# Per-unit leads and delays, feature matrices on VectorE, and an early weight load in an FNet and squared-ReLU kernel

## The chip, the core and the metric

The kernel runs on one core of a Trainium2 chip. A core has TensorE (PE in the profile; PEld is its weight load), VectorE (DVE), ScalarE (ACT), GpSimd (POOL) and SyncE (SP), which run their own instruction streams and meet by semaphores, and 16 DMA engines. DMAs are issued on the queues of SP, ACT and POOL. The metric is the time of one execution on the device in microseconds; of several runs, the median.

## What is computed

```python
def _attn_ref(x):                      # x: 8 x 3008 x 256, float32
    X = np.fft.fft(x, axis=1)
    X = np.fft.fft(X, axis=2)
    return X.real.astype(np.float32)

def _moe_ref(x, w_in, w_out):          # x: 24064 x 256, w_in: 256 x 2048, w_out: 2048 x 256
    h = np.maximum(x @ w_in, 0.0)
    return (h * h @ w_out).astype(np.float32)
```

The second function takes the first one's result, its eight batches of 3008 rows laid end to end. The output is 24064 x 256 in float32.

## The kernel before

**The transform.** The rows of a batch are folded by symmetry (`fold_ops`): sums `u` and `v` and features `w`, all on VectorE, from an `x4` tile that holds one batch and its reversed rows. The reversed rows come by indirect DMAs of POOL (`gather`, line 101), the others by direct ones (SP for batch 0, POOL for the rest). A DFT over the folded rows (`stage1_ops`, matmuls into `pf`) with cosine and sine tables `cosT`, `sinT` gives for each batch the two 128-row arrays `pt` and `qt`, of 1505 columns each. The tables have two blocks of columns, block 0 for even frequencies and block 1 for odd ones, and are computed by the kernel: range reduction on VectorE (`red`), sines on ScalarE (`trig`), and mirrored halves (`mir`, on ScalarE for block 0, on VectorE for block 1), which are scaled by per-partition vectors `alt`, `nalt`, `alt1`, `nalt1`.

**The weights.** The transform along the 256 features is not applied to the data. It is multiplied into `w_in` (`gmat`): four quarters of 512 columns are loaded (`load_w_in`, on the queue of ScalarE), cast (`gcast`) and multiplied with the feature matrices `csD`, which `dmats` makes. The results are `G1`, `G2` and `G3`, the last being `G2` with signs (`gneg`). `w_out` is loaded by POOL as float16 (`load_w_out`).

**The main loop.** The 8 x 1505 columns are cut into 25 chunks: two of 256, 22 of 512, one of 264. A chunk is passed in units: one unit is 128 of the 2048 hidden rows (256 in the two small chunks), so a full chunk has 16 units. All units in order are the steps of the loop. A unit needs the product for the columns and for their mirror images. The letter in `KINDS` says how it is made:

- `r`: `x_front` streams `G1` and `G2` into a PSUM tile `xb`, ScalarE writes the relu of it (line 607); two steps later `x_back` adds the `G3` product and ScalarE writes the mirror's relu (line 675). Three sets of matmuls.
- `v`: the same, with the mirror's relu on VectorE (line 672).
- `d`: `x_take` streams `G1` alone; VectorE forms T = X - 2 xb (line 653), where the edge product X is made by `edge` (line 634, VectorE) out of one broadcast row. Two steps later `x_back` adds the `G2` product, ScalarE writes the relu (line 663), and a mirror add on VectorE (line 664) writes the mirror's relu from xb and T. Two sets of matmuls.
- `q`: like `d`, but ScalarE copies -2 xb (line 650) and POOL adds X (line 651).
- `p`: like `d`, but POOL makes the edge product. No unit of the kernel before has it.

When the two units of a pair are there, their `h` tile is squared, on VectorE (line 687) or, for the pairs in `SQA`, on ScalarE in two halves (lines 684 and 685). Then come the 128-row matmuls with `wout16` into `po` (`mm2_ops`), which are spread over the steps of the next chunk, the copy to `os` (line 558) and the store on SP's queue.

**What sets the order.** The schedule is by hand: each engine's instructions run in the order in which the Python code issues them. Each step issues the front of its unit, half of its share of `po` matmuls, the back of the unit of two steps ago, the other half, the mirror adds that are due (`DLAG`: one step after their back), the edge product of the next step's unit, the squares that are due (three steps behind the back, one in the small chunks), and then what `side` has for this step: gmat, table operations, folds, DFT matmuls, each placed by a fraction of its batch's steps (`FOLD`, `ST1`).

**The start.** Lines 689 to 733 are the ramp, before the loop. `dmats` runs first and puts four operations and the eight of `alt_vecs` on POOL; the table operations of block 0 follow on VectorE and ScalarE in two halves, then `dmats_fin`, `sgn_vecs` on POOL, a memset of `ez`, two operations of block 1's tables, the mirrors of block 0 with the four weight loads after the second of them, the folds of batch 0 with `load_w_out` and then the load of batch 1 among them. Ten matmuls named `warm` on the zeroed `ez`, whose result nobody reads, run ahead of the first real ones, and one more behind `gmat(0)`.

Of the kernel before, what the change touches and what calls it, by code (L numbers as in the profile page):

```python
# [14 lines left out]
ALU = mybir.AluOpType  # L15
# [4 lines left out]
R23 = float(2.0 ** 23)  # L20
# [4 lines left out]
def kernel(  # L25
# [7 lines left out]
    nc = tc.nc  # L33
    B, S, D = x.shape
    _, F = moe_w_in.shape
    P = 128
# [129 lines left out]
    nalt1 = vec("nalt1")  # L166

    def alt_vecs():
        nc.gpsimd.tensor_scalar(out=alt, in0=pidx, scalar1=0.5, scalar2=-0.25, op0=ALU.mult, op1=ALU.add)
        nc.gpsimd.tensor_scalar(out=alt2, in0=alt, scalar1=R23, scalar2=None, op0=ALU.add)  # L170
        nc.gpsimd.tensor_scalar(out=alt2, in0=alt2, scalar1=R23, scalar2=None, op0=ALU.subtract)
        nc.gpsimd.tensor_tensor(alt, alt, alt2, op=ALU.subtract)
        nc.gpsimd.tensor_scalar(out=alt, in0=alt, scalar1=4.0, scalar2=None, op0=ALU.mult)
        nc.gpsimd.tensor_scalar(out=nalt, in0=alt, scalar1=-1.0, scalar2=None, op0=ALU.mult)
        nc.gpsimd.tensor_scalar(out=alt1, in0=top, scalar1=2.0, scalar2=alt[:, 0:1], op0=ALU.mult, op1=ALU.add)
        nc.gpsimd.tensor_scalar(out=nalt1, in0=alt1, scalar1=-1.0, scalar2=None, op0=ALU.mult)

    def sgn_vecs():
        nc.gpsimd.tensor_scalar(out=sgn, in0=pidx, scalar1=P - 1.5, scalar2=None, op0=ALU.is_lt)
        nc.gpsimd.tensor_scalar(out=s3, in0=sgn, scalar1=-2.0, scalar2=None, op0=ALU.mult)  # L180
        nc.gpsimd.tensor_scalar(out=sgn, in0=sgn, scalar1=2.0, scalar2=-1.0, op0=ALU.mult, op1=ALU.add)
        nc.gpsimd.tensor_scalar(out=nsgn, in0=sgn, scalar1=-1.0, scalar2=None, op0=ALU.mult)

    def absval(o, i):
        ts(out=o.bitcast(I32), in0=i.bitcast(I32), scalar1=0x7FFFFFFF, scalar2=None,
# [4 lines left out]
    sinD = csD[:, :, 1, :]  # L190

    def dmats():
        pv = nc.gpsimd
        t, m = jm[:, 1], jm[:, 2]
        pv.tensor_scalar(out=m, in0=jrow, scalar1=pidx[:, 0:1], scalar2=None, op0=ALU.mult)
        pv.tensor_scalar(out=t, in0=m, scalar1=1.0 / D, scalar2=R23, op0=ALU.mult, op1=ALU.add)
        pv.tensor_scalar(out=t, in0=t, scalar1=R23, scalar2=-float(D),
                         op0=ALU.subtract, op1=ALU.mult)
        pv.tensor_tensor(m, m, t, op=ALU.add)
        pv.memset(csD[:, 0, 0, P - 1 : P], 1.0)  # L200
        alt_vecs()

        def fin():
            absval(t, m)
            nc.vector.tensor_copy(csD[:, 0, 1, P - 1 : P], alt)
            act(csD[:, 0, 1, 0 : P - 1], m[:, 0 : P - 1], AF.Sin, bias=0.0, scale=wD)
            act(csD[:, 0, 0, 0 : P - 1], t[:, 0 : P - 1], AF.Sin, bias=hpi[:, 0:1], scale=-wD)

        def hi():
            act(csD[:, 1, :, 0:P:2], csD[:, 0, :, 0:P:2], AF.Copy, bias=0.0, scale=-1.0)  # L210
            nc.scalar.copy(csD[:, 1, :, 1:P:2], csD[:, 0, :, 1:P:2])
        return fin, hi
# [85 lines left out]
    def gcast(c, cp):  # L298
        cp(win16(c), wst[c])
# [188 lines left out]
        g += n  # L488


    KINDS = ["vrvrrrrrrrrrrrrr"] + ["rrrrvrrvrrrrrrrr"] + ["rvrrvvrrrvrrrrrr"] + ["rrrrrrrqdrrdrrrr"] + ["rdqqrrqrqrrrdrrq"] + ["rrrrddrrqrqrdqqq"] + ["rrrrrrqqqddrrdqd"] + ["rrdrqqdrrdrrqrqr"] + ["rqdddrqrrdrdrrdr"] + ["qddrqrdrrrdqddrr"] + ["drddqrdrrrddqrdr"] + ["qrrdrdddrrdrqrqr"] + ["drrdrqdrrddrdrqr"] + ["rrqdrdqrqqrrrddr"] + ["rrddqdqqrrqqdqqq"] + ["rrrrrrqqqddqrqrd"] + ["qdrdddrdqdrqdqrr"] + ["drdqqqrdqrqdrqqr"] + ["qdqqdqrqqrqdrqrq"] + ["dddrdqrdrqqdrqdq"] + ["dddrdqdrqrqdrddr"] + ["qdqqdqrdqrqdrqqr"] + ["qrqddqrqqrqdrqdr"] + ["qdqqdqvqqrqdqrdr"] + ["rddrdddddrdrdrdd"]
    SQA = [()] + [(3,)] + [(2, 6)] + [(0, 4, 5)] + [(0, 2, 5, 6)] + [(0, 4, 6)] + [(2, 3, 7)] + [(4, 6)] + [(5, 7)] + [(2, 5, 6)] + [(3, 7)] + [(0, 2, 6)] + [(0, 2, 5, 6)] + [(2, 4, 6)] + [(3,)] + [(1, 4, 6, 7)] + [(1, 2, 6)] + [(1, 4, 6)] * 2 + [(1, 4, 5, 6, 7)] + [(1, 4, 6)] * 3 + [(1, 4, 6, 7)] + [(0, 1, 6)]

    gE = const.tile([P, NFC], F16, name="gE")
    gE2 = const.tile([P, NFC], F32, name="gE2")
# [120 lines left out]
            nc.sync.dma_start(out=ebc[c][:, o : o + l],  # L616
                              in_=PQ[b][1][P - 1 : P, i : i + l].unsqueeze(1).to_broadcast([1, P, l]))

    DLAG = {'q': 1, 'd': 1, 'p': 1}
    mirrors = []  # L620
    taken = [0]
    tbuf = []
# [33 lines left out]
    def x_back(cur):  # L656
        c, u, xb, T = cur
        g0, n, nf, segs = chunks[c]
        if T is not None:
            fs = slice(u * P, (u + 1) * P)  # L660
            for (b, i, o, l) in segs:
                mm(xb[:, 0, o : o + l], G2[:, fs], PQ[b][1][:, i : i + l], False, True)
            act(r_s(c, u), xb, AF.Relu, scale=-1.0)  # L663
            mirrors.append((DLAG[KINDS[c][u]], lambda: relu_d(c, u, lambda o, i: nc.vector._custom_dve(  # L664
                TENSOR_ADD_SAT, out=o[:, 0, :], in0=xb[:, 0, i], in1=T[:, i], s0=BIG, s1=0.0))))
            return
        for j in range(nf):
            fs = slice((u * nf + j) * P, (u * nf + j + 1) * P)
            for (b, i, o, l) in segs:
                mm(xb[:, j, o : o + l], G3[:, fs], PQ[b][1][:, i : i + l], False, True)  # L670
        if KINDS[c][u] == "v":
            relu_d(c, u, lambda o, i: ts(out=o, in0=xb[:, :, i], scalar1=-1.0, scalar2=0.0,
                                         op0=ALU.mult, op1=ALU.max))
            return
        relu_d(c, u, lambda o, i: act(o, xb[:, :, i], AF.Relu, scale=-1.0))  # L675
# [14 lines left out]
    fe, fo = fold_ops(0)  # L690
    rd0, tr0, mi0 = table_ops(0)
    rd1, tr1, mi1 = table_ops(1)
    dmats_fin, dmats_hi = dmats()

    def load_w_in():
        for c in range(4):
            cs = slice(c * F // 4, (c + 1) * F // 4)
            nc.scalar.dma_start(out=wst[c],
                                in_=moe_w_in[:, cs].rearrange("(c p) f -> p c f", p=P))
# [6 lines left out]
                in_=moe_w_out[c * F // 4 : (c + 1) * F // 4, :].rearrange("(c p) o -> p c o", p=P))  # L706

    for h in range(2):
        for f in rd0[5 * h : 5 * h + 5] + (tr0[5:] if h else tr0[:5]):
            f()  # L710
    dmats_fin()
    sgn_vecs()
    nc.vector.memset(ez, 0.0)
    for f in rd1[0:2] + mi0[0:2] + [load_w_in] + mi0[2:] + fe[0:3] + rd1[2:3]:
        f()
    dmats_hi()
    warm = psx.tile([P, 512], F32, name="warm", tag="x")

    for _ in range(10):
        mm(warm, ez[:, 0, 0, :], ez[:, 0, 0:4, :], True, True)  # L720
    for f in fe[3:6] + [load_w_out] + fe[6:]:
        f()
    gcast(0, nc.scalar.copy)
    gmat(0)
    for _ in range(1):
        mm(warm, ez[:, 1, 0, :], ez[:, 1, 0:4, :], True, True)
    gcast(1, nc.scalar.copy)
    gcast(2, nc.vector.tensor_copy)
# [17 lines left out]
    for c in range(1, F // 512):  # L746
        side.setdefault(c * (c - 1) // 2, []).extend([lambda c=c: gmat(c), lambda c=c: gneg(c)])

    spread(rd1[3:], 0, 5)
    spread(fo, 8, 9)  # L750
    spread(tr1[0:5], 11, 12)
    spread(tr1[5:], 11, 13)
    spread(mi1, 12, 13)
    spread(stage1_ops(0, 1, True), 14, 15)
    FOLD = {0: [(1, 0.489, 0.896)], 1: [(2, 0.02, 0.073), (3, 0.261, 0.695), (4, 0.581, 0.851)],
            2: [(5, 0.06, 0.96)], 3: [(6, 0.04, 0.96)], 4: [(7, 0.04, 0.85)]}
    ST1 = {0: (0.9, 0.945)}
    EGRP = {1: [2, 3, 4], 4: [5, 6, 7]}
    e_done = {}
    for b in range(B - 1):  # L760
# [23 lines left out]
            side.setdefault(lead, []).append(lambda c=c: e_spread(c))  # L784

    LAG = 2
    SQ = 3
    flight = []
    made = []
    rest = []  # L790
    mmq = []
    wait = []
    due = 0

    def retire():
        v = made.pop(0)
        x_square(v)
        if v[1] == NFC // chunks[v[0]][2] - 1:
            wait.append(v[0])

    for si, (c, u) in enumerate(steps):
        while wait:
            d = wait.pop(0)
            mmq += mm2_ops(d)
            due = si + NFC // chunks[d + 1][2]
        take = [mmq.pop(0) for _ in range(-(-len(mmq) // max(1, due - si)))]
        flight.append((x_front if KINDS[c][u] in "rv" else x_take)(c, u))
        h = len(take) // 2
        posts = [f() for f in take[:h]]
        if len(flight) > LAG:  # L810
            x_back(flight[0])
            made.append(flight.pop(0))
        posts += [f() for f in take[h:]]
        due_now = [f for k, f in mirrors if k <= 0]
        mirrors[:] = [(k - 1, f) for k, f in mirrors if k > 0]
        for f in due_now:
            f()
        for p in posts:
            if p:
                p()  # L820
        while rest:
            rest.pop()()
        if si + 1 < len(steps) and KINDS[steps[si + 1][0]][steps[si + 1][1]] not in "rv":
            edge(*steps[si + 1])
        while len(made) > (1 if made and made[0][0] < 2 else SQ):
            retire()
        for f in side.get(si, []):
            f()
    while flight:
        x_back(flight[0])  # L830
        made.append(flight.pop(0))
        while mirrors:
            mirrors.pop(0)[1]()
        while made:
            retire()
    while rest:
        rest.pop()()
    for d in wait:
# [35 lines left out]
```

## Time and profile before

| | |
|---|---|
| runs | 603.01, 603.18, 603.43, 603.44, 604.67, 604.70, 605.09 us |
| median | 603.44 us |
| profiled execution | 603.25 us, of which the span is 601.5 us |
| PE, matmul | 581.3 us busy, 97% of the span, 4561 matmuls |
| ACT | 541.6 us busy, 90% |
| DVE | 526.5 us busy, 88% |
| POOL | 185.1 us busy, 31% |
| bytes moved by DMA | 56.25 MB, 94 GB/s over the span |

The span runs from the first to the last instruction of the program on the core; what lies around it is in the time of an execution, but in no view. A chain of waits follows the work that ended last back through what released it. A row of a list of waits gives the engine and what waited, what it waited for, the total in us, how many times, and the longest; a row of the timeline gives the start in us, the duration in us, the engine, the line, the operation, what it writes and reads, the shape and the count, and in brackets the idle time before it with what ended it. A group's mean mixes shapes where several forms stand in it.

### The profile page before, as it was taken

The numbers are of one execution on the slowest core, as the hardware profiler recorded it, in microseconds if no ns is written. First come the engines' busy times: TensorE is split into PE (matmuls) and PEld (weight loads), VectorE is DVE, ScalarE is ACT, GpSimd is POOL, SyncE is SP. The second block draws the span as 40 slices with busy tenths as digits, with TensorE's granted clock in tenths as the row PEclk, the third lists the DMA queues.
The fourth block names the chain that finished last, engine by engine and source line by source line (L and its number), as shares of the span: only waits on it lengthen the run. The fifth ranks groups of instructions, "written<-read, shape, count | busy, mean of one in ns | idle before, by whom it ended". The sixth has DMA issues, their size and how long they took to land.

```text
span 601.5 us, 12271 instructions
## 1 busy us (share of the span) xinstructions
PE 581.3 (97%) x4561; PEld 437.4 (73%) x4561; DVE 526.5 (88%) x954; ACT 541.6 (90%) x965; POOL 185.1 (31%) x177
## 2 busy tenths in 40 slices
PE   2899999999999999999999999999999999999997
PEld 0576677767777777777877778777787778877786
DVE  7899979998998999998889897989999989889880
ACT  5899899999998898889999989998998999999981
POOL 8502225412352014111113152322552323445300
PEclk9999999999999999999999999999999999999999
DMA  8967599673384225723133112331341422432212
GB/s 252 260 131 178 119 205 247 115 192 58 52 212 89 53 58 106 201 42 46 53 62 44 55 39 59 46 47 50 63 62 36 62 42 58 57 48 55 58 54 71
DMA packets 42337, 56.25 MB, mean 94 GB/s; under 512 B 8158, under 2 KB 37138, under 8 KB 42278
## 3 DMA queue, kind: packets, MB, share of 16 engines
q1 hardware_dynamic: 33878, 29.05, 25.9%
q0 software_dynamic: 7264, 24.31, 16.5%
q10 hardware_dynamic: 1136, 2.12, 1.0%
q8 instruction: 35, 0.57, 0.4%
q14 instruction: 24, 0.20, 0.1%
HBM read 29.02 MB, written 24.64 MB: 89 GB/s over the span
## 4 chain that ended last, share of the span: by engine, by line
PE 83%; ACT 9%; DVE 4%; POOL 1%; issue 1%; ACTq 0%; DVEq 0%; POOLq 0%
PE po L73 49%; PE xb L73 29%; PE pf L73 5%; ACT h L607 2%; ACT h L675 2%; ACT h L684 1%; ACT h L685 1%; ACT h L663 1%; ACT bs L650 1%; DVE h L664 1%; DVE v L346 1%; DVE u L334 1%; POOL x L101 1%; ACT os L558 0%; DVE bs L653 0%
## 5 line engine op out<-in xcount | busy, mean ns | idle before, releaser
L73 PE MATMUL po<-wout,h 128*128 128x256 f16 x3024 | 450.0, 272 | 0.0
L73 PEld LDWEIGHTS <-h 128*128 128x128 f16 x3024 | 286.3, 98 | 109.4 <-issue 0.4
L651 POOL TENSOR_TENSOR bs<-bs,h 128x512 f32<-128x512 f32 x99 | 132.5, 1340 | 312.9 <-ACT bs L650 213.5
L73 PE MATMUL xb<-qt,G 128*128 128x512 f16 (+11 forms) x758 | 211.4, 321 | 1.8 <-ACT h L607 0.8
L664 DVE CUSTOM_DVE_ANT_0 h<-xb,bs 128x512 f16<-128x512 f32 (+1 forms) x217 | 137.6, 643 | 23.9 <-ACT h L663 22.7
L687 DVE TENSOR_TENSOR h<-h 128x2048 f16<-128x2048 f16 (+1 forms) x122 | 150.5, 1236 | 0.4 <-ACT h L675 0.4
L73 PE MATMUL xb<-pt,G 128*128 128x512 f16 (+16 forms) x512 | 146.4, 323 | 0.8 <-DVE pt L434 0.5
L73 PEld LDWEIGHTS <-G 128*128 128x128 f16 x1270 | 121.3, 98 | 25.2 <-issue 4.1
L663 ACT ACTIVATE h<-xb 128x512 f16<-128x512 f32 (+1 forms) x206 | 129.3, 628 | 8.2 <-PE xb L73 6.4
L607 ACT ACTIVATE h<-xb 128x512 f16<-128x512 f32 (+1 forms) x178 | 110.8, 626 | 12.7 <-PE xb L73 12.2
L675 ACT ACTIVATE h<-xb 128x512 f16<-128x512 f32 (+2 forms) x174 | 105.5, 611 | 11.4 <-PE xb L73 9.3
L653 DVE SCALAR_TENSOR_TENSOR bs<-xb,h 128x512 f32<-128x512 f32 (+1 forms) x107 | 70.7, 661 | 17.7 <-PE xb L73 13.9
L634 DVE TENSOR_SCALAR h<-eb,gE 128x512 f16<-128x512 f16 (+1 forms) x206 | 79.7, 395 | 0.5 <-DMA eb<-qt 0.4
L685 ACT ACTIVATE h<-h 128x1024 f16<-128x1024 f16 (+1 forms) x70 | 75.0, 1071 | 0.0
L684 ACT ACTIVATE h<-h 128x1024 f16<-128x1024 f16 (+1 forms) x70 | 73.8, 1054 | 0.0
L558 ACT ACTIVATE os<-po 128x512 f32<-128x512 f32 x94 | 59.3, 630 | 8.7 <-PE po L73 8.6
L650 ACT ACTIVATE bs<-xb 128x512 f32<-128x512 f32 x99 | 63.7, 643 | 3.0 <-PE xb L73 1.4
L334 DVE TENSOR_TENSOR u<-x 127x765 f16<-127x765 f32 x32 | 30.6, 976 | 0.6 <-DMA x<-in_x_dram 0.6
L124 POOL DMA_DIRECT2D x<-in_x_dram x14 | 8.3, 590 | 58.9 <-DVE u L338 58.9
L73 PEld LDWEIGHTS <-w 127*128 127x128 f16 (+1 forms) x192 | 21.8, 117 | 5.6 <-DVE cosT L280 0.6
L101 POOL DMA_INDIRECT x<-in_x_dram,idx x18 | 23.4, 1298 | 5.4 <-issue 4.9
L352 DVE TENSOR_TENSOR w<-v 127x381 f16<-127x381 f16 x64 | 21.3, 358 | 0.0
(103 smaller groups left out, 226.3 us busy)
## 6 DMA issues: line engine op xcount, KB each, us to landing
out_dram<-os SPq DMA_DIRECT2D x157, 128.0 KB
x<-in_x_dram POOLq DMA_DIRECT2D x14, 756.0 KB, 10.5
wst<-in_moe_w_in_dram ACTq DMA_DIRECT2D x4, 512.0 KB
eb<-qt SPq DMA_DIRECT2D x14, 128.0 KB
x<-in_x_dram SPq DMA_DIRECT2D x2, 756.0 KB
wout<-in_moe_w_out_dram POOLq DMA_DIRECT2D x4, 256.0 KB, 5.8
x<-in_x_dram,idx POOLq DMA_INDIRECT x18, 11.1
gE<-G SPq DMA_DIRECT2D x16, 0.2 KB
```

The source lines that it names most:

```text
L73: nc.tensor.matmul(o, l, r, start=start, stop=stop, skip_group_check=True)
L607: act(r_s(c, u), xb, AF.Relu, scale=-1.0)
L634: ts(out=X, in0=ebc[c][:, 0:n], scalar1=gE2[:, u : u + 1], scalar2=None, op0=ALU.mult)
L650: act(T, xb, AF.Copy, bias=0.0, scale=-2.0)
L651: nc.gpsimd.tensor_tensor(T, T, X, op=ALU.add)
L653: stt(out=T, in0=xb, scalar=-2.0, in1=X, op0=ALU.mult, op1=ALU.add)
L663: act(r_s(c, u), xb, AF.Relu, scale=-1.0)
L664: mirrors.append((DLAG[KINDS[c][u]], lambda: relu_d(c, u, lambda o, i: nc.vector._custom_dve(TENSOR_ADD_SAT, out=o[:, 0, :], in0=xb[:, 0, ...
L675: relu_d(c, u, lambda o, i: act(o, xb[:, :, i], AF.Relu, scale=-1.0))
L684: act(h2[:, 0:nf], h2[:, 0:nf], AF.Square)
L685: rest.append(lambda: act(h2[:, nf:], h2[:, nf:], AF.Square))
L687: vt(h2, h2, h2, op=ALU.mult)
```

## The change

**The loop's tables.** `DLAG`, the fixed lead of the edge product and the fixed lag of the squares become one entry for each unit or pair:

```diff
+    LEAD = ["2222222222222222"] * 8 + ["2262222222222222"] + ["2222222222222222"] * 7 + ["2222222226222222"] + ["2222222222222222"] * 7 + ["2212222122222222"]
+    DEFER = ["1111111111111111"] * 3 + ["1111111111131111"] + ["1111111111111111"] + ["1111121111111111"] + ["1111111111111111"] * 3 + ["1111112111111111"] + ["1111111111111111"] * 9 + ["1111101111111111"] + ["1111111111111111"] * 5
+    SQLAG = ["1111"] * 2 + ["33333333"] * 7 + ["33333233"] + ["33333333"] * 14 + ["33334333"]
...
-    DLAG = {'q': 1, 'd': 1, 'p': 1}
...
-            mirrors.append((DLAG[KINDS[c][u]], lambda: relu_d(c, u, lambda o, i: nc.vector._custom_dve(
+            mirrors.append((int(DEFER[c][u]), lambda: relu_d(c, u, lambda o, i: nc.vector._custom_dve(
...
+    for si, (c, u) in enumerate(steps):
+        if KINDS[c][u] in "qdp":
+            l = int(LEAD[c][u])
+            ahead.setdefault((si - l // 2, l % 2), []).append((c, u))
...
+            if v[1] % 2:
+                squares.setdefault(si + int(SQLAG[v[0]][v[1] // 2]), []).append(v)
...
+        for v in ahead.get((si, 1), []):
+            edge(*v)
         due_now = [f for k, f in mirrors if k <= 0]
...
-        if si + 1 < len(steps) and KINDS[steps[si + 1][0]][steps[si + 1][1]] not in "rv":
-            edge(*steps[si + 1])
-        while len(made) > (1 if made and made[0][0] < 2 else SQ):
-            retire()
+        for v in ahead.get((si, 0), []):
+            edge(*v)
+        for v in squares.pop(si, []):
+            retire(v)
```

A lead of 2 is one step ahead, at the place where the edge product stood before; 6 is three steps ahead, 1 is within the unit's own step.

**The units.** Of the 384 units some 20 change their letter; the sums go from 185 r, 107 d, 99 q, 9 v (counting the 16 letters that the table also has for each of the two small chunks) to 180 r, 110 d, 99 q, 9 v, 2 p. The table shows the chunks in which they change, with the unit numbers:

| chunk | before to after |
|---|---|
| 1 | 4: v to r; 5: r to v |
| 3 | 9: r to d |
| 8 | 1: q to d |
| 11 | 4: r to d |
| 13 | 13: d to q |
| 16 | 7: d to p; 10: r to q |
| 18 | 8: q to r; 9: r to q; 13: q to d |
| 19 | 14: d to q |
| 20 | 10: q to d |
| 23 | 7: q to r; 15: r to q |
| 24 (264 columns) | 9: r to d; 12: d to p; 13: r to d |

In `SQA`, the pair that ScalarE squares in chunk 1 is 2 instead of 3, and chunk 24 gets pair 2 in addition.

**The ramp.** The vectors and the feature matrices move from POOL to VectorE, and in the program they move behind the first half of the tables (the eight vectors) and behind the second (the matrices). The first weight quarter is loaded ahead of the second half of the sines, the other three after the third mirror instead of the second. `load_w_out` moves behind the load of batch 1 and the rest of the folds. There are 14 warm matmuls instead of 10, and two instead of one behind `gmat(0)`. One table operation of block 1 less runs in the ramp.

```diff
     def alt_vecs():
-        nc.gpsimd.tensor_scalar(out=alt, in0=pidx, scalar1=0.5, scalar2=-0.25, op0=ALU.mult, op1=ALU.add)
...
+        ts(out=alt, in0=pidx, scalar1=0.5, scalar2=-0.25, op0=ALU.mult, op1=ALU.add)
...
     def dmats():
-        pv = nc.gpsimd
+        pv = nc.vector
...
-        pv.memset(csD[:, 0, 0, P - 1 : P], 1.0)
-        alt_vecs()
+        nc.gpsimd.memset(csD[:, 0, 0, P - 1 : P], 1.0)
...
     for h in range(2):
-        for f in rd0[5 * h : 5 * h + 5] + (tr0[5:] if h else tr0[:5]):
+        for f in rd0[5 * h : 5 * h + 5] + ([lambda: load_w_in(0)] + tr0[5:] if h else tr0[:5]):
             f()
+        if h == 0:
+            alt_vecs()
+    dmats_fin, dmats_hi = dmats()
     dmats_fin()
     sgn_vecs()
     nc.vector.memset(ez, 0.0)
-    for f in rd1[0:2] + mi0[0:2] + [load_w_in] + mi0[2:] + fe[0:3] + rd1[2:3]:
+    for f in rd1[0:2] + mi0[0:3] + [lambda: load_w_in(1, 2, 3)] + mi0[3:] + fe[0:3] + rd1[2:2]:
         f()
     dmats_hi()
...
-    for _ in range(10):
+    for _ in range(14):
         mm(warm, ez[:, 0, 0, :], ez[:, 0, 0:4, :], True, True)
-    for f in fe[3:6] + [load_w_out] + fe[6:]:
+    for f in fe[3:]:
         f()
+    load_w_out()
     gcast(0, nc.scalar.copy)
     gmat(0)
-    for _ in range(1):
+    for _ in range(2):
         mm(warm, ez[:, 1, 0, :], ez[:, 1, 0:4, :], True, True)
```

`sgn_vecs` moves to VectorE in the same way as `alt_vecs`. Element 6 of `fe` is the load of batch 1.

**The side work of the first steps.** `spread(ops, lo, hi)` deals operations out over the steps from `lo` on:

```diff
-    spread(rd1[3:], 0, 5)
+    spread(rd1[2:], 1, 3)
     spread(fo, 8, 9)
-    spread(tr1[0:5], 11, 12)
-    spread(tr1[5:], 11, 13)
+    spread(tr1[0:5], 10, 11)
+    spread(tr1[5:], 10, 14)
     spread(mi1, 12, 13)
     spread(stage1_ops(0, 1, True), 14, 15)
-    FOLD = {0: [(1, 0.489, 0.896)], 1: [(2, 0.02, 0.073), (3, 0.261, 0.695), (4, 0.581, 0.851)],
+    FOLD = {0: [(1, 0.471, 0.823)], 1: [(2, 0.02, 0.05), (3, 0.261, 0.695), (4, 0.581, 0.851)],
             2: [(5, 0.06, 0.96)], 3: [(6, 0.04, 0.96)], 4: [(7, 0.04, 0.85)]}
-    ST1 = {0: (0.9, 0.945)}
+    ST1 = {0: (0.86, 0.89)}
```

`rd1` and `tr1` are block 1's range reduction (VectorE) and sines (ScalarE), `mi1` its mirrors (VectorE); `FOLD` and `ST1` place the folds and the DFT of batch 1 within batch 0's steps.

## The prediction

> **What bounds the kernel now.** I read the page first, then the list of waits, the chain of waits, the timeline of the first 45 us and the busy time by windows.
>
> ```profile
> span 601.5 us, 12271 instructions
> PE 581.3 (97%) x4561; PEld 437.4 (73%) x4561; DVE 526.5 (88%) x954; ACT 541.6 (90%) x965; POOL 185.1 (31%) x177
> PE   2899999999999999999999999999999999999997
> PE 83%; ACT 9%; DVE 4%; POOL 1%; issue 1%; ACTq 0%; DVEq 0%; POOLq 0%
> ```
> PE is full from the third slice to the last, and 83% of the chain that ends last is PE. The whole list of PE's waits is short:
>
> ```profile
> PE warm L73 <- DVE ez L713: 11.4, 1, 11.4
> PE pc L73 <- ACT win L299: 1.9, 1, 1.9
> PE xb L73 <- ACT h L607: 0.8, 4, 0.3
> PE xb L73 <- DVE qt L427: 0.7, 1, 0.7
> PE xb L73 <- DVE pt L434: 0.5, 1, 0.5
> ```
> By windows, PE is busy 99.09 of 100 us from 40 to 140, everywhere from 140 to 480, and 19.76 of 20 us to 500:
>
> ```profile
> 23.00:40.00 17.00, 16.18 (x130) 12.43 (x128) 15.62 (x31) 16.87 (x36) 1.22 (x3) 1.00 0.99 198
> 140.00:480.00 340.00, 340.00 (x2706) 257.23 (x2705) 305.74 (x524) 314.13 (x546) 98.86 (x79) 1.00 0.36 70
> ```
> Columns: PE, PEld, DVE, ACT, POOL, clock, DMA share, GB/s. So only three things move the end: when PE gets its first real work, what it loses until about 43 us, and how many matmuls it streams after that. From 23 to 40 us ACT is the full engine (16.87 of 17.00), with PE 0.8 us short. Before that, the chain of waits:
>
> ```profile
> 10.39 0.22 POOL nalt L174
> 10.63 0.41 ACT cosT L279
> 12.68 0.88 ACTq L698
> 13.66 0.95 ACT cosT L279 x2
> 16.72 0.92 ACT win L299
> 17.68 0.61 PE pc L73 x2
> 21.94 0.62 DVE qt L427
> 22.60 0.50 PE xb L73 x3
> ```
> POOL's small vectors hold ACT to 10.63, four weight issues sit on ACT's queue (10.64 to 13.56), then mirrors, cast, gmat. Beside it runs DVE's chain to the features, nearly as late:
>
> ```profile
> 11.36 4.45 PE L73 MATMUL warm<-ez 128*128 128x512 f16 x10 [11.36 <-DVE ez L713]
> 14.74 1.80 DVE L334 TENSOR_TENSOR u<-x 127x765 f16<-127x765 f32 x2
> 17.89 1.16 DVE L352 TENSOR_TENSOR w<-v 127x381 f16<-127x381 f16 x4
> 18.76 1.13 PE L73 MATMUL pf<-cosT,w 127*128 127x377 f16 x6
> ```
> The second u pair starts at 14.74, the first w is ready 3.5 us later (17.89 + about 0.35 = 18.25), and pf starts at 18.76.
>
> **The change, part by part.** The profiled execution took 603.25 us (span 601.5 and 1.75 around it), 0.19 below the median, 603.44; the sum is made against 603.25.
>
> *VectorE makes the vectors and feature matrices.* DVE gets 8 + 4 instructions on 128x1: like hpl, hph, wsh, which follow at 1.37, 1.54, 1.73, some 0.17 each, 2.0 us. It gets three 128x128 scalar operations and one of two tensors: the 128x128 absval on DVE took 0.25, so 1.0 us (the two-tensor form lies between the 0.15 of a 128x1 and the 0.74 of a 128x567). It loses its two waits for POOL (1.09 before absval, 1.15 before the copy of alt, 2.24 together) and one table operation ahead of the second u pair (its start-to-start, 14.28 to 14.74, 0.46). Net +0.3: second u pair at 15.05. ez, which releases the warm matmuls, comes from 10.61 to 11.7.
>
> *ACT.* No wait for nalt, but the second half of the sines waits for DVE's table operations, which the 8 vectors push back by 1.4: mirrors from about 11.0 instead of 10.63. One of four issues (0.73 each) is gone from this place, a third mirror (0.5) runs while the other three issue: the fourth mirror at 12.9 instead of 14.18, and gcast(0) ends at 16.35 instead of 17.64. The gain of 1.3 isn't PE's: 14 warm matmuls at the 0.43 that each of the ten took last 6.0 us, from 12.4 to 18.4; if the clock doubles on the way (ten ran at 0.43; at 17.68 the next ran at full speed, so the rise lies between 15.2 and 17.7) they end at 16.8 to 17.6. Then gmat 0.86 and two warm matmuls 0.43: pf at 18.1 to 19.7. So pf starts at the later of this and the features. What does come earlier is the ACT copy of the first pf (20.33 behind gcast(1)), worth 0.1 on the way to qt.
> The Trainium skill ("TensorE: Matmul & The Clock Gate", Part 1: The HAM clock gate) says the warm-up is an amount of time in a free-running window, not a number of matmuls. The trace's single rise agrees but can't show the phase; by the rule a late window would leave gmat and pf at half speed, about 1.5 us more, and 14 matmuls in a row make that rarer than ten and a gap.
>
> *First weight quarter early.* It's issued on ACT's queue behind the first sines, 5 to 7 us, while x still flows (266 GB/s from 7 to 13.3 us); x's last gather lands at 14.52. Nothing of the kind is in the trace. Bounds: 0 if it moves in gaps; 512 KB at 266 GB/s, 1.97 us, if x waits for all of it. I take 0.8, since from 13.3 to 18.9, with the weights alone, the engines moved 359 GB/s: x alone doesn't fill them. The gather then lands at 15.3, and the second u pair starts 0.5 later than before (15.05 by DVE, 15.3 by x), and the first w is ready at 15.3 + 3.5 = 18.8. PE's own path gave 18.1 to 19.7. For the later of two that scatter I take pf at 19.15 against 18.76: **+0.4**; ACT's early copy, **-0.1**.
> The skill's "DMA: Bandwidth & Descriptors", Queues, rings and completion order, speaks against this edit: an engine takes packets from its rows in turn, so the quarter takes its share ahead of x. That would put the gather near 16.
>
> *w_out behind the next batch.* POOL is now free, so load_x(1) issues when the first u pair is done, near 15 instead of 18.87, and w_out behind it, four issues of 0.8, near 21 instead of 15.69. A queue's transfers land in order (before, the four w_out at 20.8 to 25.3, then x). The next batch's six loads, issued from 48.13, all landed by 64.24: 16.1 us. So x(1) is in at 31.1, and w_out's quarters, 1.5 apart, land at 32.6, 34.1, 35.6, 37.1. PE's first uses: 33.25 for the first, 33.90 and 34.78 for the second and third, each 0.3 later in the new order. The third is late by 0.5, in a stretch that ACT sets: **+0.1**. Bounds: 0, and if x(1) waits for all three late weight quarters (1.57 MB at 359 GB/s, 4.4), the third quarter late by 4.9. With that cover gone every late microsecond is PE's, and the units queued behind the waiting po are late next.
>
> *Tables of block 1 sooner.* Eight DVE operations over steps 1 to 2 instead of seven over 0 to 4, the sines from step 10, batch 1's fold two steps sooner. PE's first pf of block 1 waited for a mirror (0.6 on cosT) and the xb before it for ACT (0.3). I take **-0.4**; bounds -0.8 (all that PE lacks from 23 to 40) and +0.7 (one v relu, 0.68, queued behind four table operations on DVE, keeping its xb and the next unit's matmul).
>
> *Kinds.* An r unit streams three sets of matmuls, d, q and p two. In the unit starts of full chunks r takes 1.53 us of PE, d and q 1.31. Five r fewer: two d (chunks 3, 11), one q (16), net, at 0.217 each, and two in the last chunk (264 columns) at 0.11: **-0.87**, in a PE-bound stretch. Chunk 20 loses a q at unit 10, just where PE waited 0.5 in all near 494 for ACT's copy of bs and its backlog: **-0.5** (bounds 0, -0.5). The extra load: DVE gets 0.40 + 0.66 + 0.64 for each new d, ACT gives up 0.6; DVE has 34 us free from 140 to 480. A p edge on POOL isn't in the trace: between 0.7 (128x128) and 1.34 (the 128x512 add), or four times 1.02 at worst; it's off PE's path while x_back, two steps (2.6 us) on, hides it. If not, +1.5 each.
>
> *Lead, delay, lag.* The tables' ones, twos and threes reproduce the order of before. Ten entries differ; where they stand PE doesn't wait in this trace, so I put them at 0 (±0.3). The four extra warm matmuls lie ahead of the first work.
>
> Sum: +0.4 - 0.1 + 0.1 - 0.4 - 0.87 - 0.5 = -1.37: **601.9 us**.
>
> **The rivals.**
> *w_out late, slower.* One place: po of chunk 0. The three late weight quarters and x(1) are on their way together, and x(1)'s last load lands at 34 instead of 31.1, so each quarter of w_out comes 2.9 later and PE stands for 3.4 at 35 us: 601.9 - 0.1 + 3.4 = 605.2. It decides from 33.5 on. For: the transfers are back to back from 2 to 40 us (0.82 to 1.48 shares). Against: ACT, not PE, sets that stretch, and takes in some of it.
> *x held back, no change.* The gather lands at 16.5 (the full 1.97), w is ready at 20.0; pf comes 1.25 late instead of 0.4: 602.7. For: DVE now has only 0.2 to 0.5 of slack to it. Against: 359 GB/s are possible.
> *The ramp really shortens.* x isn't delayed, w is ready at 15.05 + 3.5 and pf starts at 18.55 (-0.2 instead of +0.4), and PE's 0.8 between 23 and 40 goes instead of 0.4: 601.9 - 0.6 - 0.4 = 600.9, less 0.3 if the ten entries pay: 600.6. For: ACT is 1.3 ahead. Against: DVE gets 3.0 us of work for 2.24 of waits.
>
> **Chances.** Likeliest 0.42, w_out late 0.22, x held back 0.18, ramp shorter 0.18. A measurement of this kernel can tell about 0.2%, 1.2 us, from no change: below 602.2 is faster, above 604.6 slower. The likeliest case, 601.1 to 603.0 by its own range, is faster in 0.26 of its 0.42, the same in 0.14, slower in 0.02; w_out late 0.02 the same, 0.20 slower; x held back 0.04 faster, 0.10 the same, 0.04 slower; the short ramp 0.17 faster. Together, rounded: faster 0.47, same 0.27, slower 0.26. The range reaches from 600.0 (the short ramp and 0.6 more of the unknowns) to 605.2 (w_out late); about 0.1 lies below and 0.1 above.
>
> **What would show it.** The second u pair at 15.0 to 15.4 (over 16: x held back), pf at 19.0 to 19.3, first gcast ended by 16.5; w_out's last landing near 37 and no po wait above 0.5; no PE wait near 494; PE streams 0.87 us less from 60 us on. Wrong: a PE wait that isn't in the list above, on POOL's p edge, on w_out or on DVE mirrors; or the clock still at half when gmat starts.

## The result and the profile after

The changed kernel is slower: 607.82 us median of 19 runs (606.33 to 609.46), against 604.31 us for the kernel before on the same chips (45 runs, 602.78 to 606.51). The ratio is 1.0062, with a 95% interval of 1.0054 to 1.0071. The prediction was 601.9 us, "faster" with 0.47; the result lies above its range. The profiled execution took 608.09 us with a span of 606.3, 4.8 more than the profiled one of before.

The page of the changed kernel, in the lines that were shown of before:

```profile
span 606.3 us, 12290 instructions
PE 582.3 (96%) x4560; PEld 437.9 (72%) x4560; DVE 533.9 (88%) x984; ACT 541.3 (89%) x960; POOL 177.9 (29%) x163
PE   2879999999999999999999999999999999999997
PEclk9989999999999999999999999999999999999999
PE 87%; DMA 5%; ACT 4%; DVE 3%; issue 1%; POOL 1%; ACTq 0%; POOLq 0%; DVEq 0%
```

Two things are new. The chain that ends last has 5% of DMA in it, where before it had none, and in the third slice (30 to 45 us) both PE and the granted clock have an 8. The waits of PE say which DMA (total in us, times, longest):

```profile
PE po L73 <- DMA wout<-in_moe_w_out_dram: 2.1, 1, 2.1
PE xb L73 <- DVE G L313: 1.4, 1, 1.4
PE pc L73 <- ACT win L298: 1.0, 1, 1.0
PE xb L73 <- DVE qt L426: 0.7, 1, 0.7
PE pf L73 <- DVE w L351: 0.7, 1, 0.7
PE xb L73 <- DVE h L674: 0.6, 1, 0.6
PE pc L73 <- DVE win L298: 0.6, 1, 0.6
```

Against the list of before, `pf` waits for `w`, `po` for `w_out`, `xb` for `G3` and for a relu on VectorE, and the last `pc` for a cast on VectorE. All of them are in the ramp. The windows (PE, PEld, DVE, ACT, POOL, clock, DMA share, GB/s) put sizes to it, the changed kernel first and the kernel before in the same windows second:

```profile
24.00:36.40 12.40, 9.82 (x76) 7.03 (x75) 9.30 (x18) 11.13 (x23) 1.49 (x2) 1.00 1.22 199
36.40:44.00 7.60, 5.49 (x36) 3.97 (x34) 6.99 (x14) 6.13 (x14) 0.00 (x0) 0.78 0.84 94
```
```profile
24.00:36.40 12.40, 11.92 (x99) 9.48 (x97) 11.70 (x24) 12.40 (x27) 0.23 (x1) 1.00 1.06 217
36.40:44.00 7.60, 7.22 (x54) 5.21 (x53) 6.92 (x16) 6.83 (x15) 0.00 (x0) 1.00 0.33 61
```

From 24 to 44 us PE does 112 matmuls instead of 153, ScalarE is no longer full, and from 36.4 to 44 the mean clock is 0.78. By the first matmul of each chunk, chunk 0 starts 1.1 us later than before (22.76 against 21.65), chunk 1 2.2 later (32.50 against 30.31) and chunk 2 6.2 later (50.55 against 44.34). From there the changed kernel is the quicker one: chunk 24 starts 5.1 later (570.43 against 565.36) and the span ends 4.8 later. So the ramp lost 6.2 us and the loop won 1.4.

The timeline of the changed kernel shows where the ramp's first microsecond went, and the last two; the line behind it is the first weight cast of the kernel before:

```profile
5.48 0.41 ACTq L699 DMA_DIRECT2D wst<-in_moe_w_in_dram  x1
16.23 1.82 DVE L333 TENSOR_TENSOR u<-x 127x765 f16<-127x765 f32 x2 [1.40 <-DMA x<-in_x_dram,idx]
16.63 1.04 ACT L298 CAST win<-wst 128x1024 f16<-128x1024 f32 x1 [1.31 <-DMA wst<-in_moe_w_in_dram]
19.86 1.14 PE L73 MATMUL pf<-cosT,w 127*128 127x377 f16 x6 [0.68 <-DVE w L351]
27.50 0.69 DVE L298 CAST win<-wst 128x1024 f16<-128x1024 f32 x1 [2.92 <-DMA wst<-in_moe_w_in_dram]
34.52 0.39 PE L73 MATMUL xb<-qt,G 128*128 128x256 f16 x2 [1.42 <-DVE G L313]
38.77 0.61 PE L73 MATMUL po<-wout,h 128*128 128x256 f16 x4 [2.11 <-DMA wout<-in_moe_w_out_dram]
39.73 1.01 PE L73 MATMUL po<-wout,h 128*128 128x256 f16 x4
```
```profile
16.59 1.04 ACT L299 CAST win<-wst 128x1024 f16<-128x1024 f32 x1
```

The second u pair waits for x's gather. The first weight quarter, issued at 5.48 us, gains nothing by it: its cast on ScalarE waits for it and starts at 16.63, where before, with the load issued at 10.64, it started at 16.59. The cast of the last weight quarter waits 2.92 us on VectorE, and everything in that queue behind it (the table operations of block 1, the last `G3`, a relu) comes late in this execution. Then `po` waits for `w_out`; behind that wait four `po` matmuls take 1.01 us instead of 0.60. The clock record is at half from 39.22 to 42.63 us, 3.41 us, in which PE can do 1.7 us less of matmuls; what that costs at the end is measured below.

### The profile page after: what moved, and what is told of

Same layout as the page of the kernel before. It is cut to its first block, busy times and chain, and to the rows that moved or that the text cites. A ratio compares the mean times of both kernels' runs of the same rounds, so it can differ in the third digit from the quotient of the medians.

```text
span 606.3 us, 12290 instructions
## 1 busy us (share of the span) xinstructions
PE 582.3 (96%) x4560; PEld 437.9 (72%) x4560; DVE 533.9 (88%) x984; ACT 541.3 (89%) x960; POOL 177.9 (29%) x163
## 4 chain that ended last, share of the span: by engine, by line
PE 87%; DMA 5%; ACT 4%; DVE 3%; issue 1%; POOL 1%; ACTq 0%; POOLq 0%; DVEq 0%
PE po L73 51%; PE xb L73 30%; PE pf L73 5%; DMA wout<-in_moe_w_out_dram 3%; DMA x<-in_x_dram,idx 2%; DVE u L333 1%; ACT h L677 1%; ACT h L686 1%; DVE v L345 1%; ACT h L610 1%; ACT h L687 0%; DVE h L689 0%; ACT bs L652 0%; ACT h L665 0%; POOL x L101 0%
## 5 line engine op out<-in xcount | busy, mean ns | idle before, releaser
L73 PE MATMUL xb<-qt,G 128*128 128x512 f16 (+9 forms) x752 | 210.3, 322 | 2.5 <-DVE G L313 1.4
L666 DVE CUSTOM_DVE_ANT_0 h<-xb,bs 128x512 f16<-128x512 f32 (+1 forms) x224 | 140.1, 636 | 20.5 <-ACT h L665 19.4
L689 DVE TENSOR_TENSOR h<-h 128x2048 f16<-128x2048 f16 (+1 forms) x121 | 148.4, 1231 | 0.4 <-ACT h L677 0.4
L677 ACT ACTIVATE h<-xb 128x512 f16<-128x512 f32 (+2 forms) x167 | 101.7, 613 | 11.5 <-PE xb L73 9.5
L655 DVE SCALAR_TENSOR_TENSOR bs<-xb,h 128x512 f32<-128x512 f32 (+1 forms) x112 | 73.5, 656 | 16.1 <-PE xb L73 11.7
L687 ACT ACTIVATE h<-h 128x1024 f16<-128x1024 f16 (+1 forms) x71 | 76.0, 1071 | 0.0
L686 ACT ACTIVATE h<-h 128x1024 f16<-128x1024 f16 (+1 forms) x71 | 74.9, 1055 | 0.0
L101 POOL DMA_INDIRECT x<-in_x_dram,idx x18 | 24.9, 1385 | 5.4 <-issue 4.9
```

The lines of the kernel that those rows point to most:

```text
L73: nc.tensor.matmul(o, l, r, start=start, stop=stop, skip_group_check=True)
L655: stt(out=T, in0=xb, scalar=-2.0, in1=X, op0=ALU.mult, op1=ALU.add)
L666: mirrors.append((int(DEFER[c][u]), lambda: relu_d(c, u, lambda o, i: nc.vector._custom_dve(TENSOR_ADD_SAT, out=o[:, 0, :], in0=xb[:, 0, i ...
L686: act(h2[:, 0:nf], h2[:, 0:nf], AF.Square)
L687: rest.append(lambda: act(h2[:, nf:], h2[:, nf:], AF.Square))
L689: vt(h2, h2, h2, op=ALU.mult)
```

## The experiments

**The loop's tables alone.** The ramp, its loads and the side work are those of before:

```diff
 (kernel before, in short)
-    KINDS, SQA, DLAG, SQ and the loop that goes by them
+    KINDS, SQA, LEAD, DEFER, SQLAG and the loop that goes by them
```

> The ramp, its loads and the side work of the kernel before, with the changed tables of the loop alone (kinds, ScalarE's squares, leads, delays, lags). Theory 1 (the ramp's load order lost the time; the loop gains what the prediction gave it): 0.87 us of matmuls and the 0.5 us wait near 494 us go, 1.4 us faster than before, ratio 0.9977; the start of chunk 2 stays at 44.3 us. Rival (the new delays, leads or POOL's edge products cost something in the loop): 1.000 or more.

Measured: 0.9984 (0.9969 to 0.9999), 603.85 us against 604.66; profiled 601.64 us, span 599.8, chunk 2 at 44.11. From chunk 2 to chunk 24 it takes 519.83 us, the changed kernel 519.88, the kernel before 521.02. In PE's waits after 60 us, the one near 494 us (`ACT bs`) is gone and the others stay. Theory 1 holds: in the profiles the loop's edits are a gain of about 1.4 us (0.0016 of the median here, some 1.0 us), and the whole loss lies in the ramp.

**w_out first again.** On the changed kernel, with POOL's queue held about as long as its vectors held it before (the first `w_out` load is issued at 15.03 us, before at 15.69):

```diff
...
+    gate = const.tile([P, 1], F16, name="gate")
+    nc.gpsimd.tensor_copy(gate[0:NP], uof[0][0:NP, 0, 0, 0:1])
-    for f in fe[3:]:
+    for f in fe[3:6] + [load_w_out] + fe[6:]:
         f()
-    load_w_out()
```

(`uof[0]` is the tile `u` of batch 0.)

> The changed kernel with w_out issued ahead of the next batch again, held by a one-column POOL copy until the first u pair is done, as late as it was before. Theory 1a (w_out behind x, and x ahead of the last weight quarter, lost most): PE's 2.1 us wait for w_out, the 3.4 us at half clock behind it and VectorE's 2.9 us wait for the weight quarter go; chunk 2 starts near 46 us instead of 50.5, total about 4.5 us below the changed kernel, ratio to before 0.999. Theory 2 (the early quarter is the main loss): at most 1 us better than the changed kernel, ratio 1.0045. Theory 3 (VectorE, crowded with table operations, is the main loss): PE's waits for G3 and for VectorE's relu (2.0 us) stay, ratio 1.002.

Measured: 0.9997 (0.9981 to 1.0013), 604.47 us; span 602.0, chunk 2 at 46.04. The whole list of PE's waits in the ramp behind the first:

```profile
PE xb L73 <- DVE G L313: 1.4, 1, 1.4
PE xb L73 <- DVE qt L429: 0.7, 1, 0.7
PE xb L73 <- ACT h L680: 0.3, 1, 0.3
PE pf L73 <- DVE w L353: 0.2, 1, 0.2
PE po L73 <- DVE h L692: 0.2, 1, 0.2
```

The waits for `w_out` and for the last weight quarter are gone and the clock stays full. That one edit is 0.0065 of the time, some 3.9 us: theory 1a, in its part on `w_out`. But the 1.4 us for `G3` are still there without the late quarter, so a part of theory 3 is true as well.

The other part of theory 1a, that batch 1 ahead of the last weight quarter makes it late, isn't regular. The changed kernel's profile has that cast at 27.50 us. Two experiments further down (the filling matmuls) issue the same loads in the same order and differ from the changed kernel in nothing before 34 us; this is the cast in the first of them:

```profile
23.81 0.68 DVE L298 CAST win<-wst 128x1024 f16<-128x1024 f32 x1
```

In the second it starts at 23.20, and with the side work as before at 24.54, where it waits 0.24 us. In the kernel before it started at 23.44. So the late last quarter belongs to one execution of four, and the loss doesn't rest on it: PE stood at `w_out` in that execution anyway.

The trace's DMA records show how the loads shared the engines. Packets that start in each microsecond, in the changed kernel: queue 10 carries the weights (2 KB packets), queue 0 POOL's loads (packets of x of up to 6 KB; to 14 us those of batch 0's gathers, from 18 us those of batch 1):

```
us    weights: packets, KB     x: packets, KB
12     46   94                  29  123
13     61  119                  29  166
14     82  166                  25   98
16    201  389                   0    0
17    198  391                   0    0
18    167  311                   8   49
19     41   82                  22  135
20     20   41                  36  203
21     21   43                  36  209
22     21   27                  37  221
```

Beside batch 1, the rest of the last weight quarter goes at a tenth of the pace that the weights have alone; in the kernel before the weights were through at 19 us, when `w_out` began. But at 13 and 14 us the same 2 KB packets got 119 and 166 KB beside 166 and 98 KB of the gathers, so the packets' sizes alone don't set the shares. The Trainium skill ("DMA: Bandwidth & Descriptors", Queues, rings and completion order) says that an engine takes a packet from each of its rows in turn. The trace agrees in so far as packets of both queues go in the same microsecond; one for one, by its own count, it isn't: 82 beside 25 at 14 us, 20 beside 36 at 20 us.

**The first weight quarter with the others.**

```diff
-        for f in rd0[...] + ([lambda: load_w_in(0)] + tr0[5:] if h else tr0[:5]):
+        for f in rd0[...] + (tr0[5:] if h else tr0[:5]):
...
-    ... + [lambda: load_w_in(1, 2, 3)] + ...
+    ... + [lambda: load_w_in(0, 1, 2, 3)] + ...
```

> The changed kernel with the first weight quarter loaded with the other three. Theory 2: x's last gather lands at 14.5 us instead of 16.2, pf starts near 18.8 instead of 19.86, and at least that 1.1 us is won at the end: ratio to before 1.0045 or less. Theory 1a: pf starts earlier too, but w_out still lands last, at about the same time (the same bytes lie ahead of it), and PE waits for it longer: within 0.5 us of the changed kernel, 1.0055 to 1.007.

Measured: 1.0039 (1.0023 to 1.0055), 607.12 us. The gather lands at 14.65 instead of 16.20, pf starts at 19.07, chunk 2 at 49.53. Theory 2 had the size. Of theory 1a, PE does wait longer for `w_out` (2.7 us and 0.3 instead of 2.1, with the clock at half for 3.41 us), but `w_out` doesn't land at the same time: its last quarter comes 1.0 us sooner (41.38 instead of 42.42). Batch 1 lands sooner where the gather does: its last load at 35.61 and 35.95 with gathers at 14.97 and 14.65, at 37.35 and 37.59 with gathers at 15.93 and 16.20. Its second half waits for the second u pair, and so for the gather; but its first load, issued at the same time (15.13 and 15.14), is also 0.94 sooner here, so that isn't the whole reason. In the profiles of the five kernels with the early quarter whose record has the landing, the gather landed at 14.97, 15.62, 15.84, 15.93 and 16.20; in the eight without it, between 14.10 and 15.19. So its price varies from nearly nothing to some 1.7 us. And it buys no earlier weights: in the changed kernel the first 2 KB packet starts at 9.97 us, 4.5 us behind its issue, and 256 of them, a quarter's worth, have started by 15.13; in the kernel before, with all quarters issued from 10.64 on, by 14.51.

**The side work as before.**

```diff
-    ... + fe[0:3] + rd1[2:2]:
+    ... + fe[0:3] + rd1[2:3]:
...
-    spread(rd1[2:], 1, 3)
+    spread(rd1[3:], 0, 5)
```

and `tr1`, `FOLD` and `ST1` as before.

> The changed kernel with the side work of the first steps as before (block 1's table operations over steps 0 to 4 and one of them in the ramp, its sines, the folds and the DFT of batch 1 two steps later). Theory 3: VectorE's queue is free for G3 and the relu, 2 us better than the changed kernel, ratio 1.003. Theory 1a: PE then waits for w_out that much longer, at most 0.5 us better, 1.0055 to 1.0065.

Measured: 1.0054 (1.0033 to 1.0074), 608.14 us. PE's waits for `G3` and the relu are gone, and the wait for `w_out` has grown to 4.1 us, with the clock at half for 6.83 us. The interval takes in the changed kernel's 1.0062. Whatever comes sooner ahead of a late load is waited away at the load: theory 1a, and the reason why each edit has to be judged with the load in its place.

**Two and three undone.** w_out first and the quarter late; then the side work as well; then w_out first and the side work with the early quarter kept.

> w_out ahead of the next batch as in the second experiment, and the first weight quarter loaded with the other three. Theory 2: x's last gather lands near 14.6 us, w is ready 1 us sooner, pf starts up to 0.5 us sooner than in that experiment (from then on PE's own warm matmuls set it, near 19.0), and the last weight quarter comes no later: 0.3 to 0.6 us better, ratio to before 0.999. Rival (the early quarter pays for itself: without it the cast of the first quarter waits for its load): 1.0005 or more.

> As the last, and the side work of the first steps as before, so that of the ramp's edits only the vectors and matrices on VectorE, the third mirror and the warm matmuls are left. Theory 1 + 2 + 3: no wait for w_out, G3 or a late gather; the ramp ends within 0.5 us of the kernel before, and the loop's gain of 1.4 to 1.7 us is there: ratio 0.9975. Rival (vectors and matrices on VectorE cost about 1 us by themselves): 0.999 or more.

> w_out ahead of the next batch and the side work as before, with the early quarter kept. Theory 3b (what is left of the loss with w_out in its place is eight table operations on VectorE ahead of the last G3): PE's 1.4 us wait for G3 goes, 1.4 us better than with w_out alone, ratio 0.9975. Rival (the wait for G3 came from the late weight quarter, so it stays): 0.9995.

Measured, in this order:

| | ratio to before | interval | chunk 2 | PE's wait for G3 |
|---|---|---|---|---|
| w_out, quarter | 0.9971 | 0.9958 to 0.9985 | 45.67 | 1.4 |
| w_out, quarter, side work | 0.9961 | 0.9946 to 0.9975 | 44.37 | 0 |
| w_out, side work | 0.9978 | 0.9965 to 0.9991 | 45.03 | 0 |

In the profiles the side work's placement costs the 1.3 us from 45.67 to 44.37 with nothing else in the way: eight table operations stand on VectorE ahead of the last `G3`. With w_out in its place, the early quarter costs 0.0017 to 0.0026 (0.9978 against 0.9961, 0.9997 against 0.9971), the side work 0.0010 to 0.0019 (each ratio has an interval of some 0.0014 to either side, so of these only w_out's is far outside the noise), while w_out is 0.0065. Together, along one path, 0.0101: from 1.0062 to 0.9961. With all three undone the page's third slice is full again:

```profile
span 600.1 us, 12291 instructions
PE   2899999999999999999999999999999999999997
PEclk9999999999999999999999999999999999999999
```

**Matmuls in PE's wait for w_out.** On the changed kernel, nine matmuls of 512 columns into the `po` tile, which the next matmul starts afresh. They add work and leave the result as it is.

```diff
+                if c == 0 and grp is groups[0] and j == 0 and fc == 0:
+                    for _ in range(9):
+                        mm(st["o"].rearrange("p a d -> p (a d)"), ez[:, 1, 0, :], ez[:, 1, 0:4, :], True, True)
                 mm(st["o"][0:w, j, :], h2v(c, fc // nf)[:, fc % (2 * nf), o : o + w], wout16[:, fc, :],
```

> The changed kernel with nine more 512-column matmuls on ez, into the po tile that the next matmul starts afresh, ahead of PE's wait for w_out: 1.9 us of work in the 2.1 us gap, so PE is never idle there. Theory 4 (the 2.1 us of waiting cost 1.7 us more, because the clock was at half from 39.2 to 42.6): the clock stays at full, chunk 2 starts near 49.0 instead of 50.5, ratio to before 1.0037. Rival (ScalarE and VectorE set that stretch, the half clock is hidden): within 0.5 us of the changed kernel, 1.0055 or more.

Measured: 1.0069 (1.0046 to 1.0092). The fill missed its place: `ez` had just got another writer, and the nine matmuls waited for it to 38.2, behind the gap instead of in it. The attempt still bounds a price: its clock stayed full, and from the first `po` to chunk 2 it took 10.09 us (40.16 to 50.25), the changed kernel 11.78 (38.77 to 50.55). The 1.7 us between them are the most that the half clock can have cost; in the fill, PE had been kept from its own work from 35.1 to 40.2, so that the other engines could get ahead. The kernel before, at full clock throughout, takes 11.09 for the stretch (33.25 to 44.34), only 0.7 less than the changed kernel.

With `G1` as the operand (its first 128 columns as the weights, its first 512 streamed):

> As the experiment with nine filling matmuls, with G1 as their operand, which is complete by 30 us, instead of ez, for whose writer they waited until 38.2. Theory 4 (half clock): PE works through its wait for w_out, the clock stays at full, chunk 2 starts near 49.0, 1.5 us before the changed kernel's, ratio to before 1.0037. Rival (the half clock is hidden behind ScalarE and VectorE, or the fill delays po as much as it saves): 1.0055 or more.

Measured: 1.0034 (1.0013 to 1.0056), 606.53 us; clock full, chunk 2 at 47.98 (10.99 us from the first `po`). Its interval and the changed kernel's, 1.0054 to 1.0071, just overlap; part of the better profile is luck, as the gather came early (14.97) in that execution. By the medians more PE work made the kernel faster by some 1.7 us, which is in favour of theory 4. The mean granted clock, which is on record for every execution, shows that the fill does what it was meant to: it is 0.998 or more in all nine with this fill, and 0.997 or less in 11 of the changed kernel's 19. One step of 3.41 us at half is 0.0028 of the mean. Those 11 have a median of 608.62 us, the other eight 607.18. So the half clock doesn't come in every execution, and where it comes it goes with about 1.4 us; part of that can be a longer wait ahead of it, and the stretches above put the half clock alone between 0.7 and 1.7 us.

**The number of warm matmuls.** 14 instead of 10 on the first experiment; and 10 and one instead of 14 and two on the version with three undone.

> The first experiment (the loop's tables alone on the ramp of before) with 14 warm matmuls instead of 10. Theory 5 (the kernel before has times near 603.2 and near 604.8 because in some executions ten warm matmuls and a gap of 1.9 us miss the window of the clock, and the first real matmuls run at half): the upper group goes, the spread is 1.5 us instead of 3, median ratio to before 0.9965. Rival (the spread has another cause): as in the first experiment, 0.9984, or 0.5 us worse where the four more matmuls end behind the cast.

> The version with loads and side work undone, with 10 warm matmuls and one behind gmat(0) instead of 14 and two. Theory 5: the spread of the runs grows from 1.4 to about 3 us, and the median ratio rises from 0.9961 to 0.9975. Rival (the number of warm matmuls does nothing): 0.9961; if PE's own path through 14 warm matmuls was late: 0.995.

Measured: 0.9963 (0.9950 to 0.9976) for the first, its runs within 601.41 to 602.44, where with ten they were within 601.64 to 604.99. 0.9972 (0.9960 to 0.9985) for the second, within 601.83 to 603.31. So four more warm matmuls are worth some 0.002 on the ramp of before, where ten leave a gap of 1.9 us, and at most 0.001, within the intervals, where the ten are followed after 0.8 us. The clock's rise lay anywhere from 14.9 to 17.8 us in the traces here. The mean granted clock of the executions shows that the clock is what the edit changes: it is 0.997 or less in 43 of the kernel before's 84 that were measured beside the experiments and in 6 of 12 of the first experiment, which both have ten and the gap of 1.9 us, and in none of the 12 with four more. The six have a median of 604.13 us, the other six 603.14. Theory 5 holds in kind; that the half clock lies in the ramp follows from the edit, which touches nothing else, but no profile fell on such an execution, and the upper end of the spread has another part that this doesn't explain: some executions of the kernel before take 605.6 to 606.4 us at a clock of 1.0.

**One operation less ahead of the second u pair.**

```diff
 (three undone)
-    ... + fe[0:3] + rd1[2:3]:
+    ... + fe[0:3]:
-    spread(rd1[3:], 0, 5)
+    spread(rd1[2:], 0, 5)
```

> The version with loads and side work undone, without the table operation of block 1 that stands ahead of the second u pair (it goes to step 0 of the loop). Theory: the second u pair starts at 14.8 instead of 15.2, pf at 18.4 instead of 18.8, 0.4 us better than that version: ratio to before 0.9955. Rival (PE's warm matmuls or x's last gather hold pf anyway): 0.9961 as that version.

Measured: 0.9961 (0.9949 to 0.9974), the rival's figure. In its trace the gather holds the pair to 15.08, and the warm matmuls run to 17.76, since the clock rose late; pf starts at 19.09.

**The best versions** are three that can't be told apart: 0.9961 for the changed kernel with three edits undone (602.50 us) and for the last one (602.00), and 0.9963 for the ramp of before with the loop's tables and 14 warm matmuls (602.06). They beat both kernels. In the first two VectorE makes the vectors and matrices, in the third POOL does: no run moves that edit alone, but beside the others it is worth nothing that can be seen here.

## Why the prediction was wrong

The step that failed is `w_out` behind the next batch: the sum has it at +0.1 us, and undoing it gave back 0.0065 of the time, of 0.0084 between the forecast (601.9 against 603.25, 0.9978) and the measured 1.0062. The steps, in their order:

- **VectorE's vectors and matrices**: right. ez was ready at 11.80 (predicted 12.4), and with the quarter undone the second u pair starts at 14.74 to 15.2 (predicted 15.05).
- **ScalarE and the warm matmuls**: right for the mirrors (the fourth started at 12.76; predicted 12.9), wrong for the first cast. It was to end at 16.35, 1.3 us sooner than before; it started at 16.63, because it waited 1.31 us for the weight quarter that had been issued early. So ScalarE wasn't ahead; pf was set by the features all the same.
- **First weight quarter, +0.4**: the mechanism (x is held back) was right, the size was not. The gather landed at 16.20 in the profiled execution, 1.68 late, near the upper bound, where 0.8 was taken; pf came 1.10 late. The choice from "359 GB/s are possible" failed: the average over a stretch with the weights alone says nothing of what x gets beside them.
- **w_out behind the next batch, +0.1**: this is the step that failed. x(1)'s last load was to land at 31.1 and landed at 37.59; w_out's quarters came at 38.72 to 42.42, past even the bound (x(1) at 35.5, so 37.0 to 41.5). The row for x(1) was taken from batch 2, which loads with little but stores of the output beside it: there the first load lands 6.4 us behind its issue, and the next two each 3.6 and 3.8 us behind the one before. In the ramp x(1) starts among the weights, and these are 9.9, 4.8 and 4.7 us. The kernel before had a nearer row, x(1) itself, whose second and third loads land 4.5 and 4.4 us behind the one before. The price was too low as well: 2.1 us of waiting, not 0.5, and behind it, in 11 of 19 executions, the half clock with 0.7 to 1.7 us more, which isn't in the sum at all.
- **The other direction of the same contention isn't in the sum either**: that x(1), moved ahead, can hold back the last weight quarter. In the profile it kept VectorE waiting for 2.92 us, with `G3` and the relu behind it in the queue; but of four profiles with these loads only this one has it (the others 0.24, 0 and 0), and PE waited for `w_out` behind it in any case. It explains this trace, not the median.
- **Tables of block 1 sooner, -0.4**: the wrong sign. With w_out in its place it cost 1.1 us (0.9997 against 0.9978; 1.3 in the profiles). It was costed by the PE idle time that it might remove, with one relu as the only victim; the victim was the last `G3`.
- **Kinds, -0.87 and -0.5, and the ten entries, 0**: right, and at the places named. Predicted -1.37, measured -1.4 from chunk 2 to the end: chunks 3, 11 and 16 are shorter by 0.21, 0.22 and 0.20 us, the last one with what follows it by 0.23, chunk 20 by 0.40. Another 0.17 in chunk 4 isn't in the sum. POOL's edge products made no wait.
- **The rivals**: "w_out late" named the place and 605.2; "x held back" named the other. They were weighed as alternatives with 0.22 and 0.18, but they came together, on a set of engines that is full until 40 us. What "takes in some of it" was to come from ScalarE, which sets that stretch; ScalarE ran dry instead (11.13 of 12.40 us busy, 12.40 before).

The median was 3.5 us above before's, less than the 4.8 of the two profiles: the profiled execution of before was among its quicker ones.

## What to carry to other kernels

While the DMA engines are full, issuing a load sooner needn't land it sooner: here a weight quarter issued 5 us earlier was used no earlier (16.63 us against 16.59), and it delayed the gather beside it by up to 1.7 us. So cost a moved load by what each other transfer loses, and take landing times from a stretch with the same company. A queue that looks idle may have been a timer: POOL's slow vector work kept the next batch's load behind the weights, and taking that work away moved the load. A wait of PE that lowers the clock costs more than the wait, here 0.7 to 1.7 us more, at most half of the time at half clock. And one profile is one execution: before a wait in it is made a cause, look whether other profiles with the same code up to there have it.

## What the runs showed of the hardware that was not expected

- In the 14 traces, the stretches of full and of half clock between two changes last 3.41, 6.83, 20.48, 23.89, 583.68, 587.09 or 590.51 us, which are 1, 2, 6, 7, 171, 172 and 173 times 3.413 us. So the clock changed only at steps of that length, counted from its rise. Up to chunk 2, a step at full clock in which PE was idle for 2.11, 2.71 or 3.24 us (by the records of its matmuls) was followed by half clock (the changed kernel, the late quarter, the old side work); with 1.88 us or less none was. The wait of 3.1 us in the first fill experiment left the clock full: it fell across the end of a step, with 1.76 us idle in the one and 1.34 in the next. The Trainium skill ("TensorE: Matmul & The Clock Gate", HAM oscillation — how this bites in real kernels) warns of gaps over about 3.4 us. Here 2.1 were enough where they lay within one step.
- POOL's third and fourth `w_out` loads weren't issued when their turn came, but at 25.33 and 30.09 us, 0.28 us after the first two loads of x(1) landed (25.05, 29.81); with the late quarter and with the old side work the delay is the same 0.28 to 0.29 us. So with eight loads under way, the ninth waited. They were behind x in the queue anyway. Whether the chip or the program's semaphores set that number wasn't tried.
